# Second weight blocks by a plain load and a GpSimd add, and four loads on other queues or later, in a Fourier filter with a gated MLP

## The chip, the cores and the metric

The kernel runs on one core of a Trainium2 chip. The core has TensorE (PE, the matmuls), VectorE (DVE), ScalarE (ACT), GpSimd (POOL) and SyncE (SP, which here only starts transfers), 16 DMA engines, the on-chip memory SBUF, and PSUM, in which PE accumulates. Each engine works through its own instructions in order; engines wait for one another by semaphores. A transfer is started by an instruction of an engine's queue, so what stands behind a waiting transfer on that engine waits too. The metric is the time of one execution on the device in microseconds.

## The reference

```python
x  = A_x                                   # 2048 x 1024, float32
xn = layernorm(x)                          # over the 1024 columns
s  = irfft2(rfft2(xn) * (w_r + 1j * w_i))  # 2-D, over 2048 x 1024
h  = silu(xn @ w1)                         # 1024 -> 3584
g  = silu(h @ w2)                          # 3584 -> 1024
out = x + s * g
```

## The kernel before

Every large product is made of three float16 matmuls: each float32 operand is split into a high float16 part (by ScalarE, `high`, L281) and a low one, the rest (by VectorE, `low`, L284); high by high, high by low and low by high are added in PSUM.

**First product, mm1 (0 to about 570 us).** xn is held transposed in four chunks c of 512 rows. `mm1(c, f)` makes one group of 24 matmuls (L490, output `pa`) for a chunk and a block f of 128 hidden columns; ScalarE applies silu (L499, `h`). The main loop runs over a list `order` of 112 such groups, numbered n. After each group it takes steps from three lists of background work, each a chain of Python generators: `bg` (layernorm, forward transform, filter, inverse), `wq` (the splits of w1, later of w2) and `xq` (maxima). So what an engine has to do stands in the order in which these steps were taken. The groups named in `EXTRA` take a further step of `wq`. From n = 22 on (if the layernorms are done) the loop adds the maxima of both weights (`wmax_gen`, `w2max_gen`) and, behind them in `bg`, the filter and the inverse.

`w2max_gen` loads w2 in 28 pieces (`w2m`), makes sums and differences of blocks on VectorE (`wd`, L407) and stores them to DRAM (`ws`, L408). The hidden values are combined and split as well (`hr`, `hosum`, `hoone`) and stored to DRAM as `hd` (L521). The forward transform leaves its result in DRAM as `rd`; its buffers lie in a pool A that is closed before the filter's pool B opens in the same room.

**Filter (about 555 to 837 us, `f_gen`).** 16 units u multiply the spectrum with the filter. A unit loads `vr` (L1024), `wq` (L1041), and for each quarter q a matrix `kq` (L1017; q = 0 on GpSimd's queue, the others on ScalarE's), splits `vr` into `vq` and runs the matmuls `fx` (L1053). It runs between the last mm1 groups and the first products of mm2. Its result goes to DRAM as `zd`.

**Second product, mm2 (about 570 us to the end).** A scheme of Strassen's kind: seven products m = 0 to 6, each of eight row blocks j, each in two halves k of 21 matmuls (output `pb`, L572 to L574). Product m, half k needs the tile `w2_m_k` (seven blocks of w2, split) and the tiles `ht` of the hidden values (L548). `w2_gen` makes the blocks, 14 for each m: in loop n it starts the load of block n+4 into a buffer `jr` (`load`, L444), adds the second block of w2 for block n+3 (`join`, L448, only for m = 4 and 5, where the sum isn't in `ws`), takes the high part of block n (`split`) and the low part of block n-1 (`rest`). Six `jr` buffers and four buffers of the w2 tiles go round.

**Inverse (`i_gen`, from about 905 us).** It goes over four chunks c in the order 1, 3, 0, 2, between the matmuls of m = 3 to 6. `open_i` opens its pool; `load_i` loads a chunk's spectrum `zt` (L1289) and matrix `kk` (L1293); `cis` (L1279) is the matrix of the last step. A chunk runs matmuls `iu` (L1331, L1339; six groups of 24), VectorE's steps on `ub`, `up`, `uu`, the split into `us`, and matmuls `id` with `cis` (L1420). The rows of s go to DRAM (`sd`) and are read back as `fs` (L589) where the final sum out = x + s*g is made. `switch(a, b, wait, before, lag)` is a generator that waits for the job `before`, takes `lag` empty steps, closes pool a, calls b, and takes `wait` empty steps. For the inverse:

```python
add(bg, switch(B, open_i, 6, lag=2))
```

The functions that the change touches:

Of the kernel before, what the change touches and what calls it, by code (L numbers as in the profile page):

```python
# [10 lines left out]
F16 = mybir.dt.float16  # L11
F32 = mybir.dt.float32
# [16 lines left out]
IORDER = (1, 3, 0, 2)  # L29
SUMMED = (4, 5)  # L30
TURNED = (2, 3)
EXTRA = (20, 22, 24)
ENTRY = ("fbwb||ew", "bbbwwbb|bwbb|f", "fwwbbw|wbbb|wb", "|wew|wf", "w||w")


# [115 lines left out]
def spectral_ffn(ctx, tc, x, w_r, w_i, w1, w2, ca, kc, ci, tw, pm, out):  # L151
    nc = tc.nc
# [278 lines left out]
    def w2_block(m, q, b):  # L431
        r, h = W2_BLOCKS[m][b]
        return w2[(2 * q + r) * 128:(2 * q + r + 1) * 128, h * 512:(h + 1) * 512]

    def w2_gen():

        todo = [(m, q) for m in range(7) for q in range(NP)]
        raw = {}

        def load(n):  # L440
            if n < len(todo):
                m, q = todo[n]
                raw[n] = J["p"].tile([128, 512], F32, name=f"jr{n}", tag="jr", bufs=6)
                nc.sync.dma_start(raw[n], ws[m][q] if m in ws else w2_block(m, q, 0))  # L444

        def join(n):
            if n < len(todo) and todo[n][0] in SUMMED:
                nc.gpsimd.dma_start(raw[n], w2_block(*todo[n], 1), accum_op=OP.add)  # L448

        def split(n):  # L450
            m, q = todo[n]
            if q % 7 == 0:
                w2t[m, q // 7] = fp.tile([128, 7, 2, 512], F16, name=f"w2_{m}_{q // 7}", tag="big", bufs=4)
            high(w2t[m, q // 7][:, q % 7, 0], raw[n], sc2[:, q:q + 1])

        def rest(n):
            m, q = todo[n]
            w = w2t[m, q // 7][:, q % 7]
            low(w[:, 1], raw.pop(n), sc2[:, q:q + 1], w[:, 0])
            ready2[0] = n  # L460

        for n in range(4):
            load(n)
        yield 0
        yield 0
        for n, (m, q) in enumerate(todo):
            while q % 7 == 0 and (done2[0] < m - 1 or chunks[0] <= (3 if m else q // 7) and m < 2):
                if n and ready2[0] < n - 1:
                    rest(n - 1)
                yield 0  # L470
            load(n + 4)
            join(n + 3)
            split(n)
            if n and ready2[0] < n - 1:
                rest(n - 1)
            yield 0.1
        rest(n)
# [100 lines left out]
    def rows_for(c, p, h, pool, tags):  # L578

        hsl = slice(h * 512, (h + 1) * 512)  # L580
        if (c, p) in sstore:
            sstore.pop((c, p))()
        t_ = []
        for name, src, (tag, bufs) in (("fs", sd[c, p], tags[0]), ("fx", xs[4 * c + p], tags[1])):
            if name == "fs" and (c, p) in resident:
                t_.append(resident[c, p][:, hsl])
                continue
            t_.append(tile_of(pool, [128, 512], F32, f"{name}{c}_{p}_{h}", tag, bufs))
            nc.sync.dma_start(t_[-1], src[:, hsl])  # L589
        return t_  # L590

    def ahead_rows(m, j):
# [419 lines left out]
    def f_gen():  # L1012
        bp = B["p"]

        def load_k(q):
            t_ = bp.tile([128, 4, 2, 128], F16, name=f"kq{q}", tag="K", bufs=2)
            (nc.scalar if q else nc.gpsimd).dma_start(t_, kf[q])  # L1017
            B["k"][q] = t_

        def load_v(u):  # L1020
# [252 lines left out]
    def open_i():  # L1273
        C["es"] = ExitStack()
        C["p"] = C["es"].enter_context(tc.tile_pool(name="inv", bufs=1, side="right"))
        C["ci"] = C["p"].tile([128, 2, 4, 2, 256], F16, name="cis")
        C["z"], C["k"] = {}, {}
        load_i(IORDER[0])
        nc.sync.dma_start(C["ci"], ci)  # L1279
        H["fin"] = H["es"].enter_context(tc.tile_pool(name="fin", bufs=1))  # L1280

    def load_i(c):
        zt = C["p"].tile([128, 8192], F16, name=f"zt{c}", tag="zt", bufs=1)
        if c % 2:
            src = zd[c].rearrange("(m e) q h (r x) -> r m e (q h) x", e=2, r=2)
            dst = zt.rearrange("m (e k x) -> m e k x", e=2, k=8)
            for r in range(2):
                for e in range(2):
                    nc.sync.dma_start(dst[64 * r:64 * r + 64, e], src[r, :, e])  # L1289
        else:  # L1290
            nc.sync.dma_start(zt.rearrange("m (q h x) -> m q h x", q=4, h=2), zd[c])
        k = C["p"].tile([128, 2064], F16, name=f"kk{c}", tag="kk", bufs=1)
        nc.sync.dma_start(k, ki[c])  # L1293
        C["z"][c], C["k"][c] = zt, k

    def edge_in(c):
# [8 lines left out]
    def i_gen(c):  # L1305
# [177 lines left out]
        for i in range(6):  # L1483
            if i >= 2:
                split(i - 2)
            if i < 2:
                mat(i)
            if 1 <= i <= 4:
                post(i - 1)
            yield PAUSE if i <= 3 else 3.9  # L1490
            if 1 <= i <= 2:
                mat(i + 1)
# [54 lines left out]
    with tc.manual_schedule():  # L1547
# [94 lines left out]
        for n, (c, f) in enumerate(order):  # L1642
            left -= 1
            if f == 0 and c:
                finish(bg, ln[c])
            if ln[3].done and n >= 22 and not f_job:
                add(xq, wmax_gen())
                max_job = add(xq, w2max_gen())
                f_job = add(bg, switch(A, open_f, 1, max_job))
                add(bg, f_gen())  # L1650
                add(bg, switch(B, open_i, 6, lag=2))
                for k in IORDER:
                    add(bg, i_gen(k))
            if left == 2 * LAST + 3:
                finish(wq, w1j)
                finish(xq, max_job)
                finish(bg, f_job)
                w2_scales()
                add(wq, w2_gen())
            chunks[0] = sum(last_use[k] < n for k in range(4))  # L1660
            if left == 3:
                load_h(0, 0, 0, nc.sync)
                load_h(0, 0, 1, nc.sync)
                load_h(0, 1, 0, nc.sync)
            if left == 1:
                load_h(0, 1, 1, nc.sync)
            hold[0] = left < 4
            while f not in w1t:
                slot(wq)
            if n < len(ENTRY):  # L1670
                enter = [lambda k=k: do(k) for k in ENTRY[n].split("|")]
                ev = mm1(c, f, {8: enter[0], 16: enter[1]})
                settle()
                enter[2]()
                fresh_ev[0] = ev
                tick()
                continue
            ev = mm1(c, f)
            if left == 0:
                for j, k in ((2, 0), (2, 1), (3, 0)):  # L1680
                    load_h(0, j, k, nc.sync)
            after(ev)
            if n in EXTRA or left < 4 * LAST and (NFT - 3 not in w1t or left < 20 and not w1j.done) or left < 2 * LAST and (left % 2 or left < 8):
                slot(wq)
# [83 lines left out]
```

## Time and profile before

| | |
|---|---|
| median of 3 runs | 1237.85 us (1232.93 to 1241.76) |
| profiled execution | 1239.27 us, of which the span of the trace is 1237.5 |
| mean granted clock of TensorE | 0.992 |
| busy: PE, DVE, ACT, POOL | 97%, 80%, 41%, 16% of the span |
| moved by DMA | 302.11 MB, 244 GB/s |

The profile is of one execution. A row of a group or of the timeline gives the busy time, the engine, the line of the code, the operation, its output and inputs (buffer numbers left out), their shapes, the count, and in brackets the engine's idle time before and what ended it. `SPq`, `ACTq` mean an instruction of that queue, such as a DMA's start. A row of the chain gives start, length and what ran. The waits view lists for an engine what its idle time was waiting for.

### The profile page before, as it was taken

The page shows a single profiled execution, that of the slowest core. Times are in us where ns is not written, and L with a number is a line of the kernel's source. Part 1 is how long each engine was busy: PE and PEld are TensorE (multiplying, and loading weights), DVE is VectorE, ACT ScalarE, POOL GpSimd, SP SyncE. Part 2 cuts the span into 40 slices and gives each one's busy share as a digit, 9 for nine tenths or more (in the row PEclk, how much of TensorE's full clock was granted, in tenths as well). Part 3 has the DMA queues.
Part 4 walks back from the last instruction along what each step waited for, and adds up shares of the span by engine and source line. Part 5 has one row for each costly group of instructions (what it writes and reads, how often), then busy time and mean ns, then how long its engine had stood idle before and what let it go on. Part 6 is the DMA issues. An engine that isn't in the chain of part 4 may idle for free.

```text
span 1237.5 us, 18333 instructions
## 1 busy us (share of the span) xinstructions
PE 1205.1 (97%) x6612; PEld 600.0 (48%) x6612; DVE 995.6 (80%) x1975; ACT 507.1 (41%) x688; POOL 192.9 (16%) x279
## 2 busy tenths in 40 slices
PE   8999999999999979989999999999989999999998
PEld 5544455445444534434444454445445555555555
DVE  7779977886887489649987999999246896799696
ACT  6675553355665444425454323222123232243212
POOL 3320031025002200412110111125021110000000
PEclk9999999999999989989999999999989999999999
DMA  8887697669889885896999999993998999989577
GB/s 251 186 195 197 186 277 234 189 155 276 248 270 294 225 283 150 187 220 160 195 246 248 286 232 281 232 307 121 258 333 212 329 314 330 320 291 355 196 227 269
DMA packets 281459, 302.11 MB, mean 244 GB/s; under 512 B 48244, under 2 KB 207220, under 8 KB 280980
## 3 DMA queue, kind: packets, MB, share of 16 engines
q1 hardware_dynamic: 273208, 284.08, 77.6%
q0 software_dynamic: 7440, 15.94, 7.5%
q8 instruction: 52, 0.85, 0.3%
q10 hardware_dynamic: 720, 0.92, 0.2%
q14 instruction: 39, 0.32, 0.1%
HBM read 183.94 MB, written 110.64 MB: 238 GB/s over the span
## 4 chain that ended last, share of the span: by engine, by line
PE 61%; DVE 18%; DMA 14%; SPq 2%; issue 2%; POOL 1%; ACT 1%; ACTq 0%; DVEq 0%; POOLq 0%
PE pa L490 23%; PE pb L572 11%; PE pb L573 11%; PE pb L574 11%; DMA ws<-wd 3%; DMA rd<-Rt,tws 2%; PE id L1420 2%; PE fx L1053 2%; DVE w L284 1%; DMA ht<-hd 1%; DVE wd L407 1%; DVE hoone L284 1%; DMA w1r<-in_B_w_dram 1%; DMA hd<-hosum 1%; DVE hosum L284 1%
## 5 line engine op out<-in xcount | busy, mean ns | idle before, releaser
L490 PE MATMUL pa<-xnT,w 128*128 128x512 f16 x2688 | 589.8, 381 | 5.9 <-ACT h L499 5.2
L490 PEld LDWEIGHTS <-w 128*128 128x128 f16 x2688 | 262.9, 98 | 329.9 <-issue 21.5
L572 PE MATMUL pb<-w,ht 128*128 128x512 f16 (+2 forms) x812 | 301.6, 373 | 6.2 <-DMA ht<-hd 6.2
L573 PE MATMUL pb<-w,ht 128*128 128x512 f16 (+2 forms) x812 | 301.5, 373 | 0.0
L574 PE MATMUL pb<-w,ht 128*128 128x512 f16 (+2 forms) x812 | 301.4, 373 | 0.0
L572 PEld LDWEIGHTS <-ht 128*128 128x128 f16 x812 | 79.7, 98 | 93.8 <-DMA ht<-hd 6.7
L574 PEld LDWEIGHTS <-ht 128*128 128x128 f16 x812 | 79.7, 98 | 91.8 <-issue 1.4
L573 PEld LDWEIGHTS <-ht 128*128 128x128 f16 x812 | 79.7, 98 | 87.0 <-issue 1.1
L499 ACT ACTIVATE h<-pa,s 128x512 f32<-128x512 f32 x112 | 75.1, 676 | 60.3 <-PE pa L490 47.0
L281 ACT ACTIVATE w<-jr,sc 128x512 f16<-128x512 f32 x98 | 67.7, 713 | 54.8 <-DMA jr<-in_B_w_dram 31.8
L281 ACT ACTIVATE hosum<-hr,hs 128x1536 f16<-128x1536 f32 x28 | 44.1, 1574 | 104.0 <-DVE hr L528 66.9
L284 DVE SCALAR_TENSOR_TENSOR w<-jr,sc,w 128x512 f16<-128x512 f32 x98 | 72.6, 750 | 16.8 <-ACT w L281 16.8
L281 ACT ACTIVATE hoone<-h,hs 128x2048 f16<-128x2048 f32 x28 | 55.9, 1998 | 59.0 <-DMA hd<-hoone 24.8
L284 DVE SCALAR_TENSOR_TENSOR hoone<-h,hs,hoone 128x2048 f16<-128x2048 f32 x28 | 65.7, 2347 | 11.0 <-ACT hoone L281 11.0
L1172 POOL TENSOR_TENSOR Z<-yb 128x32 f32<-128x32 f32 x64 | 35.0, 575 | 218.2 <-DVE yb L1149 203.3
L1077 ACT ACTIVATE zq<-Z,zs 128x1024 f16<-128x1024 f32 x16 | 18.4, 1148 | 96.8 <-DVE Z L1172 60.2
L284 DVE SCALAR_TENSOR_TENSOR hosum<-hr,hs,hosum 128x1536 f16<-128x1536 f32 x28 | 50.8, 1815 | 7.5 <-ACT hosum L281 7.5
L665 ACT ACTIVATE pl<-pl,c 128x512 f32<-128x512 f32 (+2 forms) x28 | 17.4, 655 | 79.7 <-DVE pl L641 42.4
L448 POOL DMA_DIRECT2D jr<-in_B_w_dram x28 | 24.4, 873 | 153.7 <-DMA jr<-in_B_w_dram 89.5
L527 DVE TENSOR_TENSOR hr<-h 128x1024 f32<-128x1024 f32 x28 | 34.2, 1222 | 14.1 <-ACT h L499 13.9
L284 DVE SCALAR_TENSOR_TENSOR w<-w1r,rs,w 128x1024 f16<-128x1024 f32 x28 | 35.7, 1277 | 9.2 <-ACT w L281 9.1
L1172 DVE TENSOR_TENSOR Z<-yb 128x128 f32<-128x128 f32 (+1 forms) x128 | 42.3, 400 | 0.0
(237 smaller groups left out, 1508.6 us busy)
## 6 DMA issues: line engine op xcount, KB each, us to landing
ht<-hd SPq DMA_DIRECT2D x112, 448.0 KB
hd<-hoone SPq DMA_DIRECT2D x28, 1024.0 KB
hd<-hosum SPq DMA_DIRECT2D x28, 768.0 KB
w1r<-in_B_w_dram SPq DMA_DIRECT2D x28, 512.0 KB
w2m<-in_B_w_dram SPq DMA_DIRECT2D x28, 512.0 KB
jr<-in_B_w_dram SPq DMA_DIRECT2D x56, 256.0 KB
ws<-wd SPq DMA_DIRECT2D x42, 256.0 KB
jr<-ws SPq DMA_DIRECT2D x42, 256.0 KB
```

Of the source, the lines that this page charges most:

```text
L281: nc.scalar.activation(hi, raw, AF.Copy, scale=scale)
L284: nc.vector.scalar_tensor_tensor(lo, raw, scale, hi, op0=OP.mult, op1=OP.subtract)
L448: nc.gpsimd.dma_start(raw[n], w2_block(*todo[n], 1), accum_op=OP.add)
L490: nc.tensor.matmul(ps, w[:, wh, d], xt[:, xh, d], start=(n == 0), stop=(n == 23))
L499: nc.scalar.activation(hq[:, 2 * (c % 2) + f % 2], ps, AF.Silu, scale=s1[:, f:f + 1])
L527: tt(sums[:, 0:2], hq[:, 0::2], hq[:, 1::2], op=OP.subtract)
L572: nc.tensor.matmul(ps, hh[:, 0], w[:, 0], start=first, stop=False)
L573: nc.tensor.matmul(ps, hh[:, 0], w[:, 1], start=False, stop=False)
L574: nc.tensor.matmul(ps, hh[:, 1], w[:, 0], start=False, stop=last)
L1053: nc.tensor.matmul(o, k[:, c, kh], v[:, c, vh], start=(n == 0), stop=(n == 2))
L1172: eng.tensor_tensor(Z[:, ns, pos], x0[:, :, ls], x1[:, :, ls], op=o_)
L1420: nc.tensor.matmul(ps[:, g, cols], us[g][:, uh, 4 * r + p], C["ci"][:, ch, g, r, cols], start=(r == 0 and n == 0), stop=(r == 1 and n == 2 ...
```

## The change

It has seven parts, all small:

1. `EXTRA` gets 21: one more step of `wq` (w1's splits) after group 21.
2. The maxima, the filter and the inverse are added from n = 21 on instead of 22.
3. A second w2 block (28 of them, for m = 4 and 5) is no longer added by a DMA of GpSimd's queue. SP loads it into the eighth slot of a w2 tile (the tiles get an eighth slot, which lies in room that their buffers have) in loop n for block n+3, and GpSimd adds it to `jr` (`add_`) in loop n for block n+1. The slot for block n+3 is that of block n+1, so the load waits for this add.
4. `kq` for q = 1 to 3 is loaded by SP's queue instead of ScalarE's.
5. `cis` is loaded at step 1 of the inverse's first chunk instead of in `open_i`, and `switch` takes five empty steps instead of six.
6. `kk` is loaded by GpSimd's queue instead of SP's.
7. `fs` rows whose store to `sd` was still held back when they are wanted are read by GpSimd's queue.

```diff
--- before.py
+++ after.py
@@ -29,7 +29,7 @@
 IORDER = (1, 3, 0, 2)
 SUMMED = (4, 5)
 TURNED = (2, 3)
-EXTRA = (20, 22, 24)
+EXTRA = (20, 21, 22, 24)
 ENTRY = ("fbwb||ew", "bbbwwbb|bwbb|f", "fwwbbw|wbbb|wb", "|wew|wf", "w||w")
 
 
@@ -435,7 +435,7 @@
     def w2_gen():
 
         todo = [(m, q) for m in range(7) for q in range(NP)]
-        raw = {}
+        raw, more = {}, {}
 
         def load(n):
             if n < len(todo):
@@ -445,12 +445,18 @@
 
         def join(n):
             if n < len(todo) and todo[n][0] in SUMMED:
-                nc.gpsimd.dma_start(raw[n], w2_block(*todo[n], 1), accum_op=OP.add)
+                spare = w2t[max(k for k in w2t if k[1] == n % 2)][:, 7].rearrange("p h x -> p (h x)").bitcast(F32)
+                nc.sync.dma_start(spare, w2_block(*todo[n], 1))
+                more[n] = spare
+
+        def add_(n):
+            if n in more:
+                nc.gpsimd.tensor_tensor(raw[n], raw[n], more.pop(n), op=OP.add)
 
         def split(n):
             m, q = todo[n]
             if q % 7 == 0:
-                w2t[m, q // 7] = fp.tile([128, 7, 2, 512], F16, name=f"w2_{m}_{q // 7}", tag="big", bufs=4)
+                w2t[m, q // 7] = fp.tile([128, 8, 2, 512], F16, name=f"w2_{m}_{q // 7}", tag="big", bufs=4)
             high(w2t[m, q // 7][:, q % 7, 0], raw[n], sc2[:, q:q + 1])
 
         def rest(n):
@@ -469,6 +475,7 @@
                     rest(n - 1)
                 yield 0
             load(n + 4)
+            add_(n + 1)
             join(n + 3)
             split(n)
             if n and ready2[0] < n - 1:
@@ -578,6 +585,7 @@
     def rows_for(c, p, h, pool, tags):
 
         hsl = slice(h * 512, (h + 1) * 512)
+        queue = nc.gpsimd if (c, p) in sstore else nc.sync
         if (c, p) in sstore:
             sstore.pop((c, p))()
         t_ = []
@@ -586,7 +594,7 @@
                 t_.append(resident[c, p][:, hsl])
                 continue
             t_.append(tile_of(pool, [128, 512], F32, f"{name}{c}_{p}_{h}", tag, bufs))
-            nc.sync.dma_start(t_[-1], src[:, hsl])
+            (queue if name == "fs" else nc.sync).dma_start(t_[-1], src[:, hsl])
         return t_
 
     def ahead_rows(m, j):
@@ -1014,7 +1022,7 @@
 
         def load_k(q):
             t_ = bp.tile([128, 4, 2, 128], F16, name=f"kq{q}", tag="K", bufs=2)
-            (nc.scalar if q else nc.gpsimd).dma_start(t_, kf[q])
+            (nc.sync if q else nc.gpsimd).dma_start(t_, kf[q])
             B["k"][q] = t_
 
         def load_v(u):
@@ -1276,7 +1284,6 @@
         C["ci"] = C["p"].tile([128, 2, 4, 2, 256], F16, name="cis")
         C["z"], C["k"] = {}, {}
         load_i(IORDER[0])
-        nc.sync.dma_start(C["ci"], ci)
         H["fin"] = H["es"].enter_context(tc.tile_pool(name="fin", bufs=1))
 
     def load_i(c):
@@ -1290,7 +1297,7 @@
         else:
             nc.sync.dma_start(zt.rearrange("m (q h x) -> m q h x", q=4, h=2), zd[c])
         k = C["p"].tile([128, 2064], F16, name=f"kk{c}", tag="kk", bufs=1)
-        nc.sync.dma_start(k, ki[c])
+        nc.gpsimd.dma_start(k, ki[c])
         C["z"][c], C["k"][c] = zt, k
 
     def edge_in(c):
@@ -1487,6 +1494,8 @@
                 mat(i)
             if 1 <= i <= 4:
                 post(i - 1)
+            if c == IORDER[0] and i == 1:
+                nc.sync.dma_start(C["ci"], ci)
             yield PAUSE if i <= 3 else 3.9
             if 1 <= i <= 2:
                 mat(i + 1)
@@ -1643,12 +1652,12 @@
             left -= 1
             if f == 0 and c:
                 finish(bg, ln[c])
-            if ln[3].done and n >= 22 and not f_job:
+            if ln[3].done and n >= 21 and not f_job:
                 add(xq, wmax_gen())
                 max_job = add(xq, w2max_gen())
                 f_job = add(bg, switch(A, open_f, 1, max_job))
                 add(bg, f_gen())
-                add(bg, switch(B, open_i, 6, lag=2))
+                add(bg, switch(B, open_i, 5, lag=2))
                 for k in IORDER:
                     add(bg, i_gen(k))
             if left == 2 * LAST + 3:
```

How the instructions stand. On ScalarE, at the end of the forward transform (`pa0_22` is mm1's group for c = 0, f = 22), before:

```order
L281 ACTIVATE hosum_0_10_1_5001<-hr10_1_4962,hs_224 128x12x128
L499 ACTIVATE h32_11_0_5004<-pa0_22_4936,s1_222 128x512
L1017 DMA kq1_5014<-in_kc_dram 128x1024
L281 ACTIVATE hoone_0_10_1_5041<-h32_10_1_4820,hs_224 128x16x128
L499 ACTIVATE h32_11_0_5004<-pa0_23_4976,s1_222 128x512
L499 ACTIVATE h32_11_0_5004<-pa1_22_5016,s1_222 128x512
```

and now on SP's queue, where the load has gone:

```order
L1032 DMA vr1_5007<-rd0_1_76 64x4x256
L1032 DMA vr1_5007<-rd1_1_80 64x4x256
L1049 DMA wq1_0_5010<-in_A_w_r_dram 128x4x128
L1049 DMA wq1_1_5012<-in_A_w_i_dram 128x4x128
L1025 DMA kq1_5014<-in_kc_dram 128x1024
L528 DMA hd_0_1_91<-hosum_0_10_1_5001 1536x1x256
L528 DMA hd_1_1_93<-hoone_0_10_1_5041 2048x1x256
```

The start of kq1's transfer stood between two activations of ScalarE and now stands between the loads of the filter's second unit and the hidden values' stores; on ScalarE `hoone` follows `h` directly.

On SP's queue, at the start of the inverse (`ht3_1_1` is the hidden tile of m = 3, j = 1, second half), before:

```order
L444 DMA jr58_8081<-in_B_w2_dram 128x512
L548 DMA ht3_0_1_8086<-hd_0_0_90 128x1792
L548 DMA ht3_1_0_8088<-hd_0_0_90 128x1792
L1289 DMA zt1_8118<-zd1_86 64x8x512 x4
L1293 DMA kk1_8123<-in_kc_dram 128x2064
L1279 DMA cis_8117<-in_ci_dram 128x4096
L444 DMA jr59_8129<-in_B_w2_dram 128x512
L548 DMA ht3_1_1_8156<-hd_0_0_90 128x1792
```

and now:

```order
L444 DMA jr58_8081<-in_B_w2_dram 128x512
L449 DMA w2_3_1_7883<-in_B_w2_dram 128x512
L555 DMA ht3_0_1_8086<-hd_0_0_90 128x1792
L555 DMA ht3_1_0_8088<-hd_0_0_90 128x1792
L1296 DMA zt1_8118<-zd1_86 64x8x512 x4
L444 DMA jr59_8128<-in_B_w2_dram 128x512
L449 DMA w2_3_0_7526<-in_B_w2_dram 128x512
L555 DMA ht3_1_1_8156<-hd_0_0_90 128x1792
```

`kk` and `cis` no longer stand between `zt` and `ht3_1_1`; a second block (written into the w2 tile, L449) stands there instead.

On PE, at the border of the two halves of m = 3, j = 1 (`pb3_1`), before:

```order
L573 MATMUL pb3_1_8271<-w2_3_0_7526,ht3_1_0_8088 128x512
L574 LDWEIGHTS ht3_1_0_8088
L574 MATMUL pb3_1_8271<-w2_3_0_7526,ht3_1_0_8088 128x512
L572 LDWEIGHTS ht3_1_1_8156
L572 MATMUL pb3_1_8271<-w2_3_1_7883,ht3_1_1_8156 128x512
```

and now:

```order
L580 MATMUL pb3_1_8275<-w2_3_0_7526,ht3_1_0_8088 128x512
L581 LDWEIGHTS ht3_1_0_8088
L581 MATMUL pb3_1_8275<-w2_3_0_7526,ht3_1_0_8088 128x512
L1338 LDWEIGHTS zt1_8118
L1338 MATMUL iu1_0_8300<-kk1_8123,zt1_8118 128x128
```

The first group of the inverse, `iu1_0`, stood behind the second half and now stands between the halves; the whole inverse comes one half product earlier.

## The prediction

> **What bounds the kernel now.** I read the busy shares first, then TensorE's (PE's) waits, then the windows in which these waits fall, then the chain that ends each.
>
> ```profile
> PE 1205.1 (97%) x6612; PEld 600.0 (48%) x6612; DVE 995.6 (80%) x1975; ACT 507.1 (41%) x688; POOL 192.9 (16%) x279
> PE s L290 <- ACT h L499: 8.3, 2, 4.5
> PE pb L572 <- DMA ht<-hd: 6.2, 1, 6.2
> ```
>
> PE is busy for 1205.1 of 1237.5 us, so only about 32 us of idle time can go, and two causes hold 14.5 of them (us in total, times, longest). But busy time also hides a loss: after a stall the matmuls run at a lower granted clock. Windows of 5 us show it (busy time and in brackets instructions of PE, its weight loads, VectorE, ScalarE, GpSimd, then the granted clock, DMA share, GB/s):
>
> ```profile
> 530.00:535.00 5.00, 5.00 (x25) 2.25 (x23) 1.97 (x2) 0.00 (x0) 0.00 (x0) 1.00 1.00 256
> 535.00:540.00 5.00, 1.70 (x8) 0.69 (x7) 2.01 (x2) 1.41 (x1) 0.67 (x1) 1.00 0.25 62
> 540.00:545.00 5.00, 3.37 (x9) 1.24 (x9) 4.33 (x5) 2.32 (x4) 0.00 (x0) 0.60 1.07 241
> 545.00:550.00 5.00, 5.00 (x18) 1.97 (x17) 1.60 (x5) 1.06 (x1) 1.36 (x2) 0.72 1.16 220
> 895.00:900.00 5.00, 2.77 (x13) 1.08 (x11) 0.83 (x2) 0.00 (x0) 0.00 (x0) 1.00 1.05 311
> 900.00:905.00 5.00, 1.05 (x3) 0.43 (x4) 0.00 (x0) 0.00 (x0) 0.86 (x1) 0.78 1.02 398
> 905.00:910.00 5.00, 5.00 (x14) 1.78 (x13) 0.00 (x0) 0.00 (x0) 0.86 (x1) 0.54 1.06 346
> ```
>
> An undisturbed window counts 25 matmuls, those over its edges included. From 535 to 550 there are 8+9+18 = 35 of 75, so (75-35)/5 = 8.0 us are lost, though the stall itself is 4.9. From 895 to 910 there are 13+3+14 = 30, so 9.0 are lost, with a stall of 6.2. A long stall thus costs about 3 more. A shorter one need not:
>
> ```profile
> 440.07 5.34 PE L490 MATMUL pa<-xnT,w 128*128 128x512 f16 x24 [3.31 <-ACT h L499]
> ```
>
> After 3.31 us of idle time 24 matmuls take 5.34 us, 0.22 each, which is the full rate (a half product of 21 takes 4.5). The change touches these two places and the stretch from 390 to 555.
>
> **The step at 537.** The change takes the load of kq1 out of ScalarE's queue.
>
> ```profile
> 538.05 0.41 ACTq L1017 DMA_DIRECT2D kq<-in_kc_dram  x1
> 538.59 2.00 ACT L281 ACTIVATE hoone<-h,hs 128x2048 f16<-128x2048 f32 x1 [20.20 <-DMA rd<-ao]
> 541.21 0.16 PE L290 MATMUL s<-m1b,unit 128*128 128x2 bf16 x1 [4.52 <-ACT h L499]
> 541.79 13.47 PE L490 MATMUL pa<-xnT,w 128*128 128x512 f16 x48 [0.41 <-ACT h L499]
> 555.61 1.36 PE L1053 MATMUL fx<-vq,kq 128*128 128x256 f16 x11 [0.24 <-DVE vq L284]
> ```
>
> The kq1 buffer lies in the room of the forward stage, so its issue waited for the last rd store (landed at 538), and hoone and h stood behind it. Without it hoone needs only the earlier store of its buffer:
>
> ```profile
> 527.36 0.57 SPq L521 DMA_DIRECT2D hd<-hoone  x1
> ```
>
> DMA traffic falls to 62 GB/s in 535 to 540, so I let that store land by 536. Then hoone runs 536 to 538, h follows, and PE goes on at about 538.8 + 0.4 instead of 541.8: a stall of 2.5, short enough for no lower clock. The 48 matmuls then take 10.4 us (0.216 each) instead of 13.5, and PE stands at fx0 at about 549.6 instead of 555.4. There the gain meets the next wait. In the row above PE came to fx0 only 0.24 us late, and what fx0 waits for is a chain of its own:
>
> ```profile
> 540.69 2.09 SPq L1024 DMA_DIRECT2D vr<-rd  x2
> 551.01 1.06 ACT L281 ACTIVATE vq<-vr 128x1024 f16<-128x1024 f32 x1 [4.46 <-DMA vr<-rd]
> 553.14 1.28 DVE L284 SCALAR_TENSOR_TENSOR w<-w1r,rs,w 128x1024 f16<-128x1024 f32 x1 [6.48 <-ACT w L281]
> 554.34 1.22 DVE L284 SCALAR_TENSOR_TENSOR vq<-vr,vq 128x1024 f16<-128x1024 f32 x1
> ```
>
> It runs from the rd stores (landed at 538, the release that held kq1) through SyncE's (SP's) load of vr1, ScalarE and VectorE to fx0, and ScalarE stood idle in it for 4.46 us. The only thing that the moved load can give it is DMA room: kq1 (256 KB at some 230 GB/s, 1.1 us) now starts behind vr1. So fx0 starts at 554.5 at best, after a new stall of 4.9 us, and the lower clock (about 2.8, the mean of the two places: 8.0-4.9 and 9.0-6.2, 2.95) follows that one instead. Net: 1.1 gained, 2.8 lost, **1.7 us slower** (from 2.8 slower, if vr1 doesn't move, to 5.5 faster, 8.0-2.5, if the chain comes as early as PE). kq2 and kq3 meet no waiting engine: the waits view has none of PE's between fx0 and 897.
>
> **w2max and the w1 step earlier.** From 385 the chain that ends in fx0 runs over DMA and VectorE, these stretches among them:
>
> ```profile
> 389.80 13.43 DMA ws<-wd
> 503.94 4.12 DMA rd<-Rt
> ```
>
> The w2max steps, of which these stores are part, come one mm1 group earlier, so one w2max step less lies in the crowded part: two sums at 0.69 on VectorE and 0.75 to 1 MB of traffic, some 3 to 4 us at the 241 and 220 GB/s of the windows above, though half of it beside work that waits anyway. PE's stalls at 436 to 450 can't be won by themselves: whatever PE gains before 555 it waits out at fx0. I take **1.5 us faster** (1.5 slower, as a piece of the forward transform now comes a group later, to 4.5 faster). Before 390 PE waits for nothing after its start, and the moved steps (n = 20 to 24) cost nothing; they would cost a stall only if VectorE, full there, held an evacuation for over two groups.
>
> **The step at 898.** SP's queue and the landing that PE waited for:
>
> ```profile
> 880.03 3.91 SPq L1289 DMA_DIRECT2D zt<-zd  x4
> 883.99 4.18 SPq L1293 DMA_DIRECT2D kk<-in_kc_dram  x1
> 889.22 14.68 DMA ht<-hd
> 898.71 0.21 DVE L1300 COPY zt<-zps 128x16 f16<-128x16 f16 x1 [4.12 <-DMA zt<-zd]
> 903.95 0.61 PE L572 MATMUL pb<-w,ht 128*128 128x512 f16 x1 [6.18 <-DMA ht<-hd]
> 911.27 1.50 PE L1331 MATMUL iu<-kk,zt 128*128 128x128 f16 x24
> 917.14 1.50 PE L1331 MATMUL iu<-kk,zt 128*128 128x128 f16 x24
> ```
>
> zt was there at 898.7, and in the 5.2 us after it kk (516 KB by its shape), cis (1024), jr (256) and ht (448), queued in this order, landed: 0.43 MB per us. The change sends kk by GpSimd's queue beside zt, cis much later, and puts iu1_0 ahead of ht3_1_1 in PE's order, just where PE fell idle (897.4). Now zt with kk beside it: 516 KB at 220 to 398 GB/s is 1.3 to 2.3 later, but the second w2 blocks, till now added within the transfer, go plainly, and the two or three of them there take from nothing to 3 off; I leave zt at 897.5 to 899.5. Behind zt stand jr, its second block and ht3_1_1, 0.96 MB or 2.2 us at 0.43, of which iu1_0's 24 matmuls cover 1.4 (1.50 with the modelled end). PE loses 1 to 3 us, taken as 2, with no stall over 3.3. 9.0 - 2 = **7 us faster** (2, if zt is so late that the stall keeps its length, to 9). cis has until the first id step, several half steps of 4.5 us on.
>
> **The adds on GpSimd.** 28 adding DMAs go, 28 second loads and 28 adds come. No wide add of GpSimd is in the trace:
>
> ```profile
> L448 POOL DMA_DIRECT2D jr<-in_B_w_dram x28 | 24.4, 873 | 153.7 <-DMA jr<-in_B_w_dram 89.5
> jr<-in_B_w_dram POOLq DMA_DIRECT2D x3, 256.0 KB, 7.3
> L1172 POOL TENSOR_TENSOR Z<-yb 128x32 f32<-128x32 f32 x64 | 35.0, 575 | 218.2 <-DVE yb L1149 203.3
> L1221 POOL TENSOR_TENSOR edge<-edge 128x16 f32<-128x16 f32 (+1 forms) x24 | 10.0, 448 | 0.5
> L407 DVE TENSOR_TENSOR wd<-w2m 128x512 f32<-128x512 f32 x28 | 19.2, 687 | 20.0 <-DMA ws<-wd 20.0
> L1172 DVE TENSOR_TENSOR Z<-yb 128x128 f32<-128x128 f32 x64 | 26.7, 477 | 0.0
> L1458 DVE TENSOR_TENSOR sk<-spa 128x128 f32<-128x128 f32 x16 | 4.7, 293 | 0.6
> ```
>
> The bounds are 0.58 (no dearer than the narrow row) and 4.4 us (by the slope, (575-448)/16 = 8 ns per element, on 480 more). I take 1.4, twice VectorE's 0.687 on that shape, the nearest row, since GpSimd's 575 is also twice VectorE's 293 on a wider one. A step of w2 takes 4.5 us (a half product) to 5.9 (917.14-911.27, with an inverse group), so GpSimd keeps up (28 x 1.4 = 39 us). The new wait is SP's: a second load waits until the add two steps before has read the same room, and jr, ht and the rows stand behind it. A load lands in about 7.3 us (the last figure of the second row, of the adding ones), with the add 8.7, against two steps of 9 to 11.8: no wait, and a jr ahead has four steps. What the adds cost VectorE, the Z rows show: beside GpSimd 477 ns instead of 293, or 64 x 0.184 = 11.8 us in GpSimd's 35, a third. 13 us in all, against
>
> ```profile
> 900.00:950.00 50.00, 46.05 (x272) 23.29 (x273) 31.72 (x80) 14.05 (x21) 10.43 (x12) 0.93 0.94 277
> 950.00:1000.00 50.00, 50.00 (x365) 28.42 (x363) 38.59 (x103) 14.20 (x29) 5.92 (x7) 1.00 1.06 311
> 1000.00:1050.00 50.00, 50.00 (x311) 26.28 (x309) 40.89 (x100) 13.60 (x27) 6.37 (x8) 1.00 0.98 323
> ```
>
> 150-111.2 = 38.8 us of VectorE's idle time. So 0. The fs rows by GpSimd move a wait of some 6 us from SP to GpSimd, with an add behind: 0.
>
> Sum: -1.7+1.5+7 = 6.8 faster. The profiled execution took 1239.27, 1.77 beyond its span; less 6.8 it is 1232.5, and as the median stands 1.4 below it, **1231**.
>
> **The rivals.** *The chain to fx0 gives way*: 5.5 in place of -1.7 and w2max up to 4.5; with 7 that is 17, or 1221; with half the w2max, 1223. For it: ScalarE and VectorE work sooner. Against it: the 4.46 wait for vr. *The stall at 898 only changes its name* to zt: gain 2, sum 1.8, 1236. For it: DMA is full there. *Slower, VectorE held by the adds*: if an add of 1.4 blocks VectorE for its whole length, 28 x 1.4 = 39 us fill the 38.8 that are idle, and from there each further 0.1 us an add costs 2.8. At 2.2 us an add that is 61-38.8 = 23, less 6.8: 1254. Against it, the third in the Z rows. The Trainium skill, "SBUF — State Buffer", section "SBUF: two separate sides", says that a VectorE operation with two SBUF inputs and a GpSimd one that reads SBUF exclude each other for a whole instruction; 477 against 293 is a slowdown of this kind, though a partial one on average, and by the rule this rival is the outcome. *It doesn't act* (the order is shifted, but landings set the same times): 1238.
>
> **How the numbers follow.** Forecast 0.50 (1227 to 1235), chain gives way 0.22, zt 0.15, slower 0.08, no effect 0.05. About 1%, 12 us, is what a measurement can tell from no change. Faster by over 1% (below 1225.5) is most of the first rival and a tail of the forecast: 0.26; slower (above 1250.2) 0.06; within 0.68. The range leaves out the slow case and the ends: 1219 to 1242.
>
> **What would show it.** A stall of PE before fx0 near 550 of 4 to 5 us and about 2 at 537; iu1_0 where ht3_1_1 was, and under 3 us idle there at a clock of 1.00; adds of about 1.4 us; SP's second loads without waits; VectorE's mean for 128x512 near 690 still. I am wrong if fx0 starts more than 3 us earlier, if SP waits for an add, or if VectorE's share above passes 95%.

## The result and the profile after

The changed kernel takes 1229.13 us (median of 6 runs, 1228.0 to 1230.94), the kernel before 1236.26 (6 runs, 1232.93 to 1241.76): a ratio of 0.9939, 95% interval 0.9916 to 0.9962, or about 7.5 us less. The forecast was a median of 1231, a gain of 6.8. The profiled execution after took 1228.43 us, its span 1226.5; against the span before this is 11 us, more than between the medians, because the profiled execution before was one of its slower runs.

PE's waits after, in the waits view (us in total, times, longest):

```profile
PE fx L1061 <- DVE vq L284: 5.2, 1, 5.2
PE s L290 <- ACT h L506: 4.2, 2, 3.2
PE pa L497 <- ACT h L506: 4.0, 3, 2.4
PE id L1427 <- DVE us L1417: 1.7, 2, 0.9
```

The wait for `ht` (6.2 before) is gone, the waits for `h` are shorter, and a new one has come, of 5.2 us at `fx`. The timeline after shows how it came:

```profile
532.64 2.00 ACT L281 ACTIVATE hoone<-h,hs 128x2048 f16<-128x2048 f32 x1 [18.30 <-DMA hd<-hoone]
535.27 0.16 PE L290 MATMUL s<-m1b,unit 128*128 128x2 bf16 x1 [1.02 <-ACT h L506]
535.85 10.52 PE L497 MATMUL pa<-xnT,w 128*128 128x512 f16 x48 [0.41 <-ACT h L506]
547.05 1.06 ACT L281 ACTIVATE vq<-vr 128x1024 f16<-128x1024 f32 x1 [5.07 <-DMA vr<-rd]
551.65 2.51 PE L1061 MATMUL fx<-vq,kq 128*128 128x256 f16 x11 [5.17 <-DVE vq L284]
```

`hoone` now starts when the store of its own buffer has landed, ahead of the last `rd` rows; PE waits 1.02 + 0.41 us, and its 48 matmuls take 10.52 us instead of 13.47. Then it stands at `fx0`, 5.17 us, for the landing of `vr1`, and that group of 11 runs in 2.51 us instead of 1.36. The windows at both places (same columns as before):

```profile
545.00:550.00 5.00, 1.48 (x8) 0.60 (x7) 0.82 (x1) 2.09 (x2) 0.00 (x0) 0.93 1.14 264
550.00:555.00 5.00, 3.35 (x14) 2.07 (x14) 1.78 (x3) 3.40 (x4) 0.00 (x0) 0.50 1.09 318
555.00:560.00 5.00, 5.00 (x23) 2.10 (x21) 5.00 (x5) 3.31 (x4) 0.00 (x0) 0.89 0.27 69
895.00:900.00 5.00, 5.00 (x43) 3.00 (x42) 1.82 (x3) 1.21 (x2) 2.10 (x2) 1.00 1.03 400
900.00:905.00 5.00, 5.00 (x43) 3.00 (x42) 3.12 (x4) 2.10 (x4) 2.74 (x3) 1.00 1.03 377
905.00:910.00 5.00, 5.00 (x43) 3.00 (x42) 4.93 (x16) 1.57 (x3) 1.83 (x2) 1.00 0.99 386
```

From 895 to 910 PE is busy without a gap, at a clock of 1.00: none of the 9.0 us is lost. The lower clock that stood at 540 now follows the wait at `fx0`. Last, the adds, and the busy times:

```profile
PE 1202.3 (98%) x6612; PEld 600.1 (49%) x6612; DVE 1015.4 (83%) x1975; ACT 505.9 (41%) x688; POOL 206.3 (17%) x285
L454 POOL TENSOR_TENSOR jr<-jr,w 128x512 f32<-128x512 f32 x28 | 38.7, 1385 | 107.6 <-DMA w<-in_B_w_dram 60.2 <-DVE w L284 16.3 <-DVE up L1365 10.3
SPq L449 <- POOL jr L454: 9.7, 5, 5.5
```

An add takes 1.385 us on average. VectorE is busy for 1015.4 us instead of 995.6 with the same 1975 instructions: 19.8 us more, for GpSimd's 38.7. SP waits five times for an add, 9.7 us in all, and PE, in its waits above, waits for none of the transfers that stand behind them. VectorE's share in the stretch of the adds (same columns):

```profile
900.00:950.00 50.00, 49.14 (x333) 26.79 (x332) 47.18 (x102) 17.06 (x30) 15.02 (x11) 1.00 0.82 259
950.00:1000.00 50.00, 50.00 (x321) 26.39 (x320) 43.13 (x100) 10.84 (x20) 12.18 (x10) 1.00 0.97 337
1000.00:1050.00 50.00, 49.13 (x314) 26.17 (x313) 45.37 (x96) 13.50 (x27) 9.34 (x10) 1.00 0.92 329
```

VectorE is idle for 14.3 of these 150 us, against 38.8 before; its share is 94% in the fullest window, just under the 95% that the prediction named as a sign of being wrong.

### The profile page after: what moved, and what is told of

It reads as the page before. It is cut to its first block, busy times and chain, and to the rows that moved or that the text cites. A ratio compares the mean times of both kernels' runs of the same rounds, so it can differ in the third digit from the quotient of the medians.

```text
span 1226.5 us, 18352 instructions
## 1 busy us (share of the span) xinstructions
PE 1202.3 (98%) x6612; PEld 600.1 (49%) x6612; DVE 1015.4 (83%) x1975; ACT 505.9 (41%) x688; POOL 206.3 (17%) x285
## 4 chain that ended last, share of the span: by engine, by line
PE 46%; DMA 9%; DVE 7%; SPq 2%; issue 1%; ACT 1%; POOL 0%; DVEq 0%; POOLq 0%; ACTq 0%
PE pa L497 12%; PE pb L581 10%; PE pb L579 10%; PE pb L580 10%; PE fx L1061 2%; PE id L1427 1%; DMA w<-in_B_w_dram 1%; DMA rd<-Ro 1%; DMA ws<-wd 1%; DMA fs<-sd 1%; DMA rd<-Rt,tws 1%; DMA hd<-hosum 1%; DMA fx<-in_A_x_dram 1%; DMA ht<-hd 1%; DMA sd<-s 1%
## 5 line engine op out<-in xcount | busy, mean ns | idle before, releaser
L454 POOL TENSOR_TENSOR jr<-jr,w 128x512 f32<-128x512 f32 x28 | 38.7, 1385 | 107.6 <-DMA w<-in_B_w_dram 60.2
L281 ACT ACTIVATE w<-w1r,rs 128x1024 f16<-128x1024 f32 x28 | 31.9, 1141 | 25.5 <-DVE w L284 19.7
```

The costliest lines, as they stand in the source:

```text
L281: nc.scalar.activation(hi, raw, AF.Copy, scale=scale)
L454: nc.gpsimd.tensor_tensor(raw[n], raw[n], more.pop(n), op=OP.add)
```

## What can be compared between single profiles

The time of the first part differs between executions. (In the kernel before, the last matmul of mm1 starts at 648.6 and the first of mm2 at 648.8 us, so the two products meet there and not near 570, as the description of the kernel has it.) The start of the first `pb` matmul (the number after the comma), in three profiles of kernels whose program is the same up to 837 us (the kernel before, then the experiments b_inverse and b_w5 below):

```profile
L572 PE MATMUL pb<-w,ht x812: 219/379/634, 648.8 to 1232.6; 128*128 128x512 f16 x154, 128*128 128x128 f16 x6, 128*128 128x256 f16 x3
L572 PE MATMUL pb<-w,ht x812: 219/379/634, 643.3 to 1218.9; 128*128 128x512 f16 x154, 128*128 128x128 f16 x6, 128*128 128x256 f16 x3
L572 PE MATMUL pb<-w,ht x812: 219/379/634, 644.3 to 1221.8; 128*128 128x512 f16 x154, 128*128 128x128 f16 x6, 128*128 128x256 f16 x3
```

With b_adds below (655.6) these are 643.3 to 655.6. So I compare the **second part**, from the first `pb` to the span's end, between profiles (before 1237.5 - 648.8 = 588.7, after 1226.5 - 647.0 = 579.5), and whole times only by the ratios of many runs. The two parts aren't independent: the filter starts in the first and runs on into the second, so a first part that ends earlier can make the second longer (a_vq below is such a case). A difference of 2 or 3 us between second parts is therefore not evidence by itself. All ratios below are to the kernel before; a difference between two of them has an interval of about 4 us to either side.

## The experiments

**Each part alone, on the kernel before.** Theory: the loads and places of parts 5 and 6 carry the gain at 898; the rest is near zero, part 4 a small loss. The rival is that the adds cost, or are needed.

b_inverse, parts 5 and 6:

```diff
-        nc.sync.dma_start(C["ci"], ci)            # in open_i; now in i_gen, i == 1
-        nc.sync.dma_start(k, ki[c])
+        nc.gpsimd.dma_start(k, ki[c])
-                add(bg, switch(B, open_i, 6, lag=2))
+                add(bg, switch(B, open_i, 5, lag=2))
```

> The kernel before with parts 5 and 6 alone (cis late, five empty steps, kk by GpSimd's queue). My theory: the stall at 898 goes by these, so 8 to 9 us faster than before (about 1228), with PE busy through 895 to 910 and the rest of the trace as before, the stall at 537 included. Rival (the plain second loads and adds are needed for it, since the adding transfers keep zt late): 2 to 5 us faster, with a PE wait of iu1_0 for zt or kk of over 2 us.

Measured: 0.9928 (0.9903 to 0.9953), 8.9 us faster, as much as the whole change. Second part 580.7, 8.0 less than before. PE waited 2.4 us at iu1_0; I put that down to this execution's first part, 5.5 shorter than before's, but didn't test it. The gain needs neither the adds nor the plain loads, and none of the other five parts is shown to add to it.

b_w5, the place in PE's order alone:

```diff
-                add(bg, switch(B, open_i, 6, lag=2))
+                add(bg, switch(B, open_i, 5, lag=2))
```

> The kernel before with five empty steps alone: the inverse comes a half product earlier, the loads stay where they were. If the place in PE's order is most of the gain, 4 to 9 us faster than before. If the queue is needed too, PE stalls at iu1_0 for kk (behind zt) by 2 to 5 us and then for ht3_1_1 (behind cis) by 1 to 4, at a lower clock: 0 to 4 us faster than before.

Measured: 0.9962 (0.9941 to 0.9984), 4.7 faster; second part 582.4. The time lies in the range of the first case (4 to 9), though its interval (2.0 to 7.3) reaches into the second. The timeline shows both waits of the second case, that for kk under its 2 to 5 us, that for ht within its 1 to 4:

```profile
894.57 1.50 PE L1331 MATMUL iu<-kk,zt 128*128 128x128 f16 x24 [1.35 <-DMA kk<-in_kc_dram]
898.88 0.39 PE L572 MATMUL pb<-w,ht 128*128 128x512 f16 x1 [2.81 <-DMA ht<-hd]
```

So the order alone gives about half. The other half, 4.2 us with an interval of about 0 to 8, comes with taking kk and cis out of the way, and these two waits, 4.2 us together, agree with it. The loads without the earlier place, and without the adds, were not run.

b_kq, part 4:

```diff
-            (nc.scalar if q else nc.gpsimd).dma_start(t_, kf[q])
+            (nc.sync if q else nc.gpsimd).dma_start(t_, kf[q])
```

> The kernel before with part 4 alone (kq1 to kq3 by SP's queue). My theory: the stall at 537 shrinks to under 2.5 us, PE waits 4 to 5.5 us at fx0 instead, and the time is 0 to 3 us longer than before. Rival (the chain to fx0 comes earlier as well): 4 to 6 us shorter, with a wait at fx0 under 1 us.

Measured: 0.9992 (0.9972 to 1.0011): from 3.5 us faster to 1.4 slower, which leaves out the rival's 4 to 6. The stall at 537 is 2.4 us, and PE waits 3.4 at fx0. The exchange of one wait for the other is what the theory said; whether the sum is a small loss the runs can't tell.

b_early, parts 1 and 2:

```diff
-EXTRA = (20, 22, 24)
+EXTRA = (20, 21, 22, 24)
-            if ln[3].done and n >= 22 and not f_job:
+            if ln[3].done and n >= 21 and not f_job:
```

> The kernel before with parts 1 and 2 alone (a w1 step more, maxima and filter added one group earlier). My theory: 1 to 4 us faster, all of it between 385 and 556, fx0 starting that much earlier, the stall at 537 as before. Rival (the earlier step collides with the forward transform): the same or up to 2 us slower, fx0 not earlier.

Measured: 0.9986 (0.9965 to 1.0007): from 4.3 faster to 0.9 slower. The first `pb` starts at 646.7, inside the scatter of the old order. Not settled by itself.

b_adds, part 3:

```diff
-                nc.gpsimd.dma_start(raw[n], w2_block(*todo[n], 1), accum_op=OP.add)
+                spare = w2t[...][:, 7]...            # eighth slot of a w2 tile
+                nc.sync.dma_start(spare, w2_block(*todo[n], 1))
...
+            add_(n + 1)                               # nc.gpsimd.tensor_tensor
```

> The kernel before with part 3 alone (second blocks by a plain load, added by GpSimd). My theory: the same within 2 us; adds of 1.4 us, VectorE's busy time 13 to 20 us more, PE's waits in the inverse within 1 us of before; at 898 zt lands 0 to 3 earlier and the stall for ht stays (4 to 6 us). Rival (VectorE is held and the inverse becomes its chain): 3 us or more slower, with PE waiting for us or ub.

Measured: 1.0054 (1.0029 to 1.0078), 6.7 us **slower**: the rival. Second part 593.9, 5.2 more than before, and PE's waits in it are the ones that the rival named (the profile is of an execution of 1251.25 us, against a median of 1245.08, so they may be larger here than usual):

```profile
PE iu L1346 <- DVE ub L1355: 4.9, 1, 4.9
PE iu L1338 <- DVE ub L1355: 3.2, 1, 3.2
PE pb L579 <- DMA ht<-hd: 3.1, 1, 3.1
```

VectorE became late. The stall for ht is half of before's, but that doesn't show that the plain loads bring zt and ht sooner: with the old loads it is 4.5 us in b_kq and 6.8 in b_early, and here PE's first part was 6.8 longer than before's.

**How the adds hold VectorE.** After, in the timeline, one add and what VectorE did:

```profile
921.46 0.41 DVE L1365 TENSOR_TENSOR up<-ub 128x256 f32<-128x256 f32 x1
921.79 0.41 DVE L1366 TENSOR_TENSOR up<-ub 128x256 f32<-128x256 f32 x1
921.95 1.38 POOL L454 TENSOR_TENSOR jr<-jr,w 128x512 f32<-128x512 f32 x1 [2.69 <-DVE up L1365]
922.13 1.35 DVE L1369 TENSOR_TENSOR uu<-up 128x128 f32<-128x128 f32 x1
923.40 0.28 DVE L1370 TENSOR_TENSOR uu<-up 128x128 f32<-128x128 f32 x1
```

An operation of 0.28 us takes 1.35, until the add ends. Per line of code (minimum/median/maximum in ns):

```profile
L1380 DVE TENSOR_TENSOR ub<-up x8: 279/286/1891, 907.5 to 1007.8; 128x128 f32<-128x128 f32 x8
L1387 DVE SCALAR_TENSOR_TENSOR uu<-ub,up x32: 277/285/1359, 907.8 to 1009.8; 128x128 f32<-128x128 f32 x32
L1355 DVE TENSOR_TENSOR ub<-iu,uc x16: 674/681/685, 902.5 to 1148.0; 128x512 f32<-128x512 f32 x16
L1440 DVE TENSOR_TENSOR sk<-id,sc x16: 671/677/683, 941.0 to 1187.4; 128x504 f32<-128x504 f32 x16
```

The first two lines read both operands from SBUF, and single instances last as long as an add. The last two read one of their operands (`iu`, `id`) from PSUM, and none of them is longer than the others, though adds ran beside some: the add at 941.47 us beside both `sk` operations of 941.03 and 941.63. Instance by instance, in the trace after: nine operations with an operand in PSUM overlap an add and stay within 5 ns of their line's median; what the overlapping ones exceed their medians by is 20.6 us in all, which accounts for the 19.8 of the busy time. This is the rule of the Trainium skill, "SBUF — State Buffer", section "SBUF: two separate sides": a VectorE operation with two SBUF inputs and a GpSimd operation that reads SBUF exclude each other for the whole instruction. The trace agrees, 1.35 us instead of 0.28.

a_add2, the cost doubled, on the changed kernel:

```diff
-                nc.gpsimd.tensor_tensor(raw[n], raw[n], more.pop(n), op=OP.add)
+                spare = more.pop(n)
+                nc.gpsimd.tensor_tensor(raw[n], raw[n], spare, op=OP.add)
+                nc.gpsimd.tensor_tensor(spare, spare, spare, op=OP.add)
```

> The changed kernel with a second add on GpSimd behind each of the 28 (the spare block added to itself, its result unused): double the suspected cost. If VectorE is held for the length of an add whenever it has two operands in SBUF, VectorE's busy time grows by another 15 to 20 us, and as it is at 94% in 900 to 950 already, PE waits for us or ub: 4 to 15 us slower than the changed kernel. If the adds cost VectorE nothing that counts, within 2 us of it.

Measured: 1.0071 (1.0051 to 1.0091), 1.3% or some 16 us slower than the changed kernel. That is at the upper end of the expected 4 to 15. VectorE's busy time is 1032.0, another 16.6 us, and PE waits for the split of `us`:

```profile
PE id L1429 <- ACT us L1418: 7.1, 2, 4.1
PE id L1429 <- DVE us L1419: 2.4, 2, 1.6
```

**Parts taken out of the changed kernel.** The parts alone multiply to 0.996 (0.9928 x 0.9992 x 0.9986 x 1.0054), the whole is 0.9939; with four intervals in the product these two aren't told apart. Does the whole hide the adds, or pay for them?

a_accum, part 3 undone (the diff of b_adds backwards):

> The changed kernel with part 3 undone (second blocks again added by DMA). Theory A (the adds hold VectorE for about 20 us and this costs PE time, as it cost some 7 us when part 3 was alone): 3 to 7 us faster than the changed kernel (1222 to 1226). Theory B (with the inverse a half product earlier VectorE has the slack, and the held time falls beside PE's work): within 2 us of the changed kernel (1227 to 1231), VectorE's busy time 20 us lower all the same.

Measured: 0.9938 (0.9915 to 0.9960), the same as the changed kernel (within 4 us to either side): theory B. VectorE is busy for 995.1 us, 20 less, and PE's only wait after 860 us is 0.9. Second part 577.6, 1.9 less than the changed kernel, which is about what two profiles differ by. In the changed kernel 20 us of VectorE's time cost PE little or nothing.

a_wait6, the half product given back, all else as changed:

```diff
-                add(bg, switch(B, open_i, 5, lag=2))
+                add(bg, switch(B, open_i, 6, lag=2))
```

> The changed kernel with six empty steps again: the inverse is back at its old place in PE's order, the loads keep their new queues and places. If the queue was what mattered (kk and cis ahead of ht3_1_1), ht3_1_1 comes by 898 to 900 and PE waits 0 to 3 us: 0 to 3 us slower than the changed kernel. If the order mattered most, PE waits 4 us or more for ht: 5 to 9 us slower.

Measured: 1.0001 (0.9979 to 1.0022): the whole gain is gone, 7 us or so slower than the changed kernel. The expectation gave both cases a wait for ht as the place, and there it is 1.3 us, the first case. The time is the second's. PE's other waits in the inverse:

```profile
PE id L1427 <- DVE us L1417: 1.9, 2, 1.0
PE id L1427 <- ACT us L1416: 1.6, 2, 1.3
PE pb L579 <- DMA ht<-hd: 1.3, 1, 1.3
```

Second part 584.2, 4.7 more than the changed kernel; PE's waits behind 860 us are 5.0 instead of 2.6, which is about half of that, and the rest isn't located. Does the earlier place make the room for the adds? This run can't say, since the place was worth 4.7 us without any adds (b_w5). PE's waits for results of the inverse's vector steps (`ub`, `us`, `sk`) speak against the place alone: they are 11.1 us in b_adds, 3.7 here and 2.6 in the changed kernel, and b_adds and this run share the old place. They differ in parts 1, 2 and 4 to 7, the loads of kk and cis among them. Which part makes the room is open; the new loads with the old place and no adds, or the adds with the early place and the old loads, would tell.

a_cis, cis back in open_i, the earlier place kept:

```diff
         load_i(IORDER[0])
+        nc.sync.dma_start(C["ci"], ci)
```

> The changed kernel with cis loaded in open_i again, ahead of ht3_1_1; the inverse keeps its new place. 1024 KB at 0.4 MB/us is 2.5 us more for ht3_1_1, of which iu1_0's group covers 1.4 at most. If the queue mattered: a PE wait of 1 to 4 us at the second half of m = 3, j = 1, and 1 to 6 us slower than the changed kernel. If the order mattered most: no wait over 1 us there, and the same within 1 us.

Measured: 0.9968 (0.9949 to 0.9986), about 3.6 us slower than the changed kernel (by the two intervals from nothing to 7), with a PE wait of 2.6 us for ht at the second half of m = 3, j = 1: the first case.

**Where the gain of part 4 goes, and whether it can be had.** In the changed kernel fx0 waits for `vr1`, though it only reads `vq0`: ScalarE's splits of vq0, vq1 and w stand in this order, and VectorE's low part of vq0 stands behind that of w.

a_vq:

```diff
         high_v(0)
-        high_v(1)
         yield PAUSE
         low_v(0)
+        high_v(1)
         load_v(2)
```

> The changed kernel, with vq1's high part issued behind vq0's low part, so that fx0 no longer waits for the landing of vr1. Theory A (fx0's wait of 5.2 us and the lower clock after it are where the gain of part 4 went): fx0 starts by 547, no wait there, 5 to 8 us faster than the changed kernel. Theory B (h stands behind hosum, which waits for its buffer's store until about 551 in any case): PE then waits for h instead and the gain is 0 to 3 us.

Measured: 0.9941 (0.9920 to 0.9961), no faster than the changed kernel. Neither theory: fx0 runs at 549.4 without a wait, and the first `pb` starts at 642.7 instead of 647.0 (at 641.9 in both kernels below that share the edit; 647.0 at the earliest in five without it), so 4.3 us are there at 643. They are lost by 902: about 1 before PE comes to iu1_0, 2.2 in the wait there, and 1.8 in the lower clock behind it (the second group of the inverse starts at 902.30, in the changed kernel at 901.69):

```profile
894.35 0.21 DVE L1307 COPY zt<-zps 128x16 f16<-128x16 f16 x1 [14.06 <-DMA w<-in_B_w_dram]
894.66 1.63 PE L1338 MATMUL iu<-kk,zt 128*128 128x128 f16 x24 [2.16 <-issue]
890.00:895.00 5.00, 2.84 (x19) 1.31 (x18) 0.65 (x2) 0.00 (x0) 0.00 (x0) 1.00 1.07 299
895.00:900.00 5.00, 5.00 (x32) 2.47 (x30) 1.53 (x3) 1.20 (x2) 2.44 (x2) 0.66 1.03 395
```

In the changed kernel the same copy ran at 894.64, and iu1_0 ran at 895.82, without a wait. PE is earlier and zt isn't, nor is the filter's end that zt is made of. The last split of `zq` (the second of the two times), in the changed kernel and in a_vq:

```profile
L1085 ACT ACTIVATE zq<-Z,zs x16: 1137/1148/1151, 576.5 to 861.4; 128x1024 f16<-128x1024 f32 x16
L1085 ACT ACTIVATE zq<-Z,zs x16: 1137/1149/1151, 577.4 to 859.8; 128x1024 f16<-128x1024 f32 x16
```

It starts 1.6 us earlier with a first part 4.3 shorter: the filter's end, behind which zt comes, doesn't follow PE.

a_vq_zt and a_vq_act, two edits to bring zt sooner on top of it:

```diff
-                    nc.sync.dma_start(dst[64 * r:64 * r + 64, e], src[r, :, e])
+                    (nc.scalar if r and c == IORDER[0] else nc.sync).dma_start(...)   # a_vq_zt
+                    (nc.scalar if c == IORDER[0] else nc.sync).dma_start(...)         # a_vq_act
-                add(bg, switch(B, open_i, 5, lag=2))
+                add(bg, switch(B, open_i, 6, lag=1))                                  # a_vq_act
```

> The changed kernel with vq1 behind vq0's low part, and with two of the four pieces of the first zt (those of partitions 64 to 127) started from ScalarE's queue, beside SP's two for partitions 0 to 63. In the run with vq1 moved alone PE came to iu1_0 some 4 us sooner, but zt landed at 894 as before, with DMA full at only 200 GB/s from 880 to 892. If that rate comes of one half of the partitions being written at a time, both halves together bring zt 3 us or more earlier: no wait at iu1_0, 3 to 6 us faster than the changed kernel (1223 to 1226). If it comes of the small pieces that zt is read in, zt lands where it did and the time is that of the changed kernel within 2 us.

Measured: 0.9927 (0.9899 to 0.9955), 1227.29 us, not told apart from the changed kernel. iu1_0 ran at 894.8, where it did, with a wait of 0.6 only, since PE had waited 2.3 us for the filter's `vq` by then:

```profile
671.45 1.36 PE L1061 MATMUL fx<-vq,kq 128*128 128x256 f16 x11 [0.75 <-DVE vq L284]
688.08 1.36 PE L1061 MATMUL fx<-vq,kq 128*128 128x256 f16 x11 [1.57 <-DVE vq L284]
```

At these places the filter's chain over VectorE sets the pace.

> The changed kernel with vq1 behind vq0's low part, with all four pieces of the first zt on ScalarE's queue, and open_i one step earlier (lag 1, six empty steps, so the inverse's matmuls keep their place): SP's loads no longer stand behind zt, and zt starts as soon as zd is stored, about 872 instead of 876. If zt's 2 MB are bound by their start, zt is there by 891, PE doesn't wait at iu1_0, and the time is 3 to 5 us under that of the changed kernel (1224 to 1226). If they are bound by what DMA moves beside them, zt lands at 894 again and the time is within 2 us of it. If zt in front delays ht3_0_1 or ScalarE's last blocks for m = 3, PE waits there and it is 2 to 6 us slower.

Measured: 0.9950 (0.9929 to 0.9972), some 1.4 us slower than the changed kernel, which the intervals don't tell from nothing. The wait is that of the third case: the start of zt's four pieces took 14.5 us of ScalarE's queue, PE waited 2.7 us for ht, then 4.2 more at iu1_0, which came at 903.1:

```profile
876.16 14.51 ACTq L1296 DMA_DIRECT2D zt<-zd  x4
877.69 6.08 SPq L555 DMA_DIRECT2D ht<-hd  x2
```

I read both long starts as loads held back by the transfers already queued, which wasn't tested. The end of the wait at iu1_0 shows something else:

```profile
901.72 1.26 POOL L454 TENSOR_TENSOR jr<-jr,w 128x512 f32<-128x512 f32 x1 [5.71 <-issue]
901.99 1.05 DVE L1307 COPY zt<-zps 128x16 f16<-128x16 f16 x1 [7.24 <-DMA ht<-hd]
```

The copy took 1.05 us, until the add ended. In the thirteen other profiles, with no add beside it, it takes 0.20 to 0.21. So here an operation of VectorE with one input in SBUF, a copy, was held too. What zt's rate hangs on stays open; neither run brought it sooner. No version was shown to beat the changed kernel.

## Why the prediction was right, and where not

- **Sum.** Forecast 6.8 us less, measured 7.5 (4.7 to 10.4). Two terms in it were of the wrong size or for the wrong reason, and the term of nothing for the adds held only in company with the other parts.
- **The step at 898**, forecast 7 (2 to 9): the stall and its clock are gone entirely, 9.0 in the windows, and parts 5 and 6 alone measure 8.9 (5.8 to 12.0). Mis-sized by 2. PE did not lose the 1 to 3 us that I left: the copy behind zt ran at 894.64, ahead of my 897.5 to 899.5 (1.8 of it is the shorter first part), and ht3_1_1 was there. The step also laid the gain to the queue and counted the place in PE's order only as 1.4 us of cover. By b_w5 the place alone gives 4.7, about half. The rival that the stall only changes its name to zt didn't come true here, but where PE came sooner it shows: 2.4 us at iu1_0 in b_inverse, 2.2 in a_vq.
- **The adds**, forecast 0: right for the whole (a_accum), wrong as a property of the adds. The duration was right (1.4 forecast, 1.385). The step that failed is "a third": I took the mean slowdown of the Z rows and got 13 us for VectorE; it lost 19.8, half of the adds' 38.7. The Z rows were misread as well: one by one in the trace before, the 54 that overlap a GpSimd row take 480 to 507 ns and the ten that don't 376 to 407, so beside GpSimd they lose 0.11 each and not 0.184, some 6 us in GpSimd's 35. The share read rightly would have given 7 us, further from the 19.8: that 13 came as near was luck. GpSimd's Z rows are short (0.46 us in the median); an add takes 1.385, for the whole of which VectorE can be held, as shown above. The mechanism of the rival that I gave 0.08 is what happens when part 3 stands alone (+6.7 us, not its +16). In the whole it came to nothing; which of the other parts makes the room I had not asked, and a_wait6 leaves it open.
- **SP's second loads**, forecast no wait: there were five, 9.7 us, and no wait of PE followed from them. Part 7, the fs rows, forecast 0, was not run by itself.
- **The step at 537**: stall 1.4 (forecast 2.5), 48 matmuls 10.52 (10.4), wait at fx0 5.17 (4.9), and the lower clock behind it. The mechanism is shown step by step. The condition "short enough for no lower clock" wasn't put to the test at 1.4 us, and it isn't safe: in a_accum a wait of 2.09 us at the same place is followed by 12.21 us for these 48 matmuls (last section). The term of -1.7 isn't shown: part 4 alone lies between -1.4 and +3.5, which leaves it just outside.
- **w2max earlier**, forecast 1.5: part alone between -0.9 and +4.3; it can't be told from nothing. fx0 starts 3.96 us earlier than before, over the 3 that I named as a sign of error, but with the old order it starts at 550.1 to 562.3 in four executions, so that sign was worth nothing. What does show: in the five profiles with parts 1, 2 and 4 and without vq1 moved, the first pb starts at 647.0 to 649.7; in the four of the old order at 643.3 to 655.6. The mean is the same (648.2 and 648.0), as the forecast sum of these two terms (-0.2) had it.
- **The rival "the chain gives way"** priced a removed wait at fx0 at 5.5 us. a_vq brought the first pb 4.3 earlier, and zt, which didn't come earlier, and the lower clock behind the wait for it took it back. This follow-on I hadn't named for the rival; in this kernel its 1221 wasn't reached even with the wait at fx0 gone.

## What to carry to other kernels

A GpSimd operation that reads SBUF can cost VectorE up to its whole length, wherever VectorE's operations have two SBUF operands; here 28 adds cost it half of their time. Whether that costs anything depends on the slack of the consumer: the same adds made one kernel 6.7 us slower and cost another little or nothing. So measure such a part alone and within the whole. The place of other work in the waiting engine's order was worth about half of the gain here, and with the transfers queued ahead of the awaited one taken away it was the whole. Where single executions differ by more than the effect, compare a stretch of the trace that starts at one event, and leave the sum to many runs.

## What was not expected of the hardware

- The lower clock doesn't follow from a stall's length alone. The stall at 537 in a_vq_act and then in a_accum, with the same work behind it:

```profile
537.62 0.16 PE L290 MATMUL s<-m1b,unit 128*128 128x2 bf16 x1 [2.08 <-ACT h L506]
538.20 10.52 PE L497 MATMUL pa<-xnT,w 128*128 128x512 f16 x48 [0.42 <-ACT h L506]
536.98 0.16 PE L290 MATMUL s<-m1b,unit 128*128 128x2 bf16 x1 [2.09 <-ACT h L499]
537.56 12.21 PE L490 MATMUL pa<-xnT,w 128*128 128x512 f16 x48 [0.41 <-ACT h L499]
```

  The first runs at full rate, the second loses 1.7 us, with a granted clock of 0.77 in 540 to 545 against 1.00. Before, 3.31 us at 437 were followed by 24 matmuls in 5.34 us, the full rate; in a_vq 2.16 us at 892, with short matmuls (128x128) behind, by a clock of 0.66 in 895 to 900. What else decides was not tried.
- The copy of a_vq_act above: one input in SBUF, and held for an add all the same.
- The spread of the runs was small with the change (1228.0 to 1230.94 in 6 runs, against 1232.93 to 1241.76 in 6 of the kernel before beside them and 1231.0 to 1242.9 in 31 others). Without the adds (a_accum) it was 1225.3 to 1231.5, but in a_vq_zt 1223.3 to 1234.25, also in 6 runs; whether the change makes it smaller isn't shown.
